# All five engines in written order, and attention reordered into a pipeline of four stages

## The chip, the cores and the metric

The kernel runs on one core of one Trainium2 chip. A core has a matrix engine (TensorE, PE in the profile, with its weight loads as PEld), a vector engine (VectorE, DVE), a scalar engine (ScalarE, ACT), a general engine (GpSimd, POOL) and a queue engine that issues transfers (SyncE, SP). The metric is device time in microseconds (us), lower is better.

## The reference

Windowed attention with a few global keys and a distance bias, followed by a mixture of experts in which each token goes to one expert.

```python
B, H, S, D = 4, 8, 768, 64                 # n_global 8, n_local 96, all fp32
scores = q @ k.T / sqrt(D)
rel = pos[:, None] - pos[None, :]
is_global = pos[None, :] < n_global
is_local = (rel >= 0) & (rel < n_local)
keep = is_global | is_local
dist = where(is_global & ~is_local, n_local, abs(rel))
scores = where(keep, scores - slopes[h] * dist, -1e9)      # slopes[h] = 2 ** -(h + 1)
a = exp(scores - max); a = a / (sum(a) + 1e-9)
x = (a @ v) as (3072 tokens, 512)

logits = x @ w_gate                        # 8 experts
e = argmax(logits); g = softmax(logits)[e]
out[token] = g * (relu(x[token] @ w1[e]) @ w2[e])          # 512 -> 1024 -> 512
```

## The kernel before

**Attention** (`banded`) goes over 24 blocks of 128 queries, six for each of the four batches. Only the keys of the same block and of a mixed tile (96 keys of the block before and 32 global ones) can matter, so a block needs two 128 by 128 score tiles for each of eight heads. For block n, `scores` makes 16 matmuls in two groups of PSUM (`sp`, the array split into halves of 64 rows), VectorE adds the bias (`p<-sp`) and ScalarE takes the exponential. `prep_q` and `prep_k` transpose the next block's q and k on TensorE through a PSUM tile `pt`, and ScalarE copies out `qt`, VectorE `kt`; GpSimd then builds the mixed key tile `ka`. `values` multiplies with v (`po`, 64 columns), ScalarE copies `ot`; sums and gate logits go into `pr` (`one_in` and `gate_w` matmuls, 32 columns), ScalarE copies `rs`; `px` and a transposed `rs` bring the result to tokens as rows; VectorE divides by the sums and writes the rows `xr`. The PSUM tiles `pt` and `px` take turns in two buffers (tag "t").

The loop's order is: `scores(n)`, `prep(n+1)`, `values(n-1)` with its transposes at once. After six blocks `choose` picks an expert for every token, `dispatch` turns that into row numbers with twelve small matmuls, and GpSimd scatters the rows into a table in DRAM by indirect transfers.

**Bias tiles**: VectorE makes distance and mask for three 128 by 128 forms, seven operations each, and then for each form and head one more (L317, 24 in all).

**Experts**: the first 128 tokens of an expert are handled by `up_s` and `down_s`, the rest by one `pass` per expert, whose width (a multiple of 32) is chosen at run time by a switch. `x_in_s` and `x_in` transpose gathered rows. The weights of experts 0 and 1 are fetched during attention, 4 transfers of 1 MB each; `ys` is the one buffer from which the results of `down_s` are scattered.

**Order**: only TensorE runs in the order in which the code is written (`manual_schedule(engines={PE})`). For the other engines a scheduler places every instruction, by its own estimate of when it can run; an engine still executes its instructions strictly one after the other. `judge` reduces a per-block flag `ok`, which VectorE updates twice in every block, to one number that decides on a general fallback (it is never taken here).

Of the kernel before, what the change touches and what calls it, by code (L numbers as in the profile page):

```python
# [15 lines left out]
PE = mybir.EngineType.PE  # L16
SP = mybir.EngineType.SP
# [3 lines left out]
def kernel(  # L21
# [40 lines left out]


# [4 lines left out]
                   allow_small_or_imprecise_dtypes=True)  # L68
    col = const.tile([P, P], F32, name="col")
    nc.gpsimd.iota(col[:], pattern=[[1, P]], base=0, channel_multiplier=0,  # L70
                   allow_small_or_imprecise_dtypes=True)
    before = const.tile([P, P], BF16, name="before")
    nc.vector.tensor_scalar(before[:], col[:], iota_p[:, 0:1], None, ALU.is_gt)
    ones = const.tile([P, P], BF16, name="ones")
    nc.vector.memset(ones[:], 1.0)
# [7 lines left out]
    wg = const.tile([P, NDC, E], F32, name="wg")  # L83
    nc.scalar.dma_start(out=wg[:], in_=moe_w_gate.rearrange("(c p) e -> p c e", p=P))


    words = const.tile([P, 2, 2], I32, name="words")
    nc.scalar.dma_start(out=words[:, 0, :], in_=n_global.bitcast(I32).partition_broadcast(P))
    nc.scalar.dma_start(out=words[:, 1, :], in_=n_local.bitcast(I32).partition_broadcast(P))
# [11 lines left out]

    ok = const.tile([P, H], F32, name="ok")
    okn = const.tile([P, 3], F32, name="okn")
    nc.vector.tensor_scalar(okn[:, 0:1], ng, float(GW), None, ALU.is_le)
    nc.vector.tensor_scalar(okn[:, 1:2], nl, float(LW), None, ALU.is_le)
    nc.vector.scalar_tensor_tensor(okn[:, 2:3], nl, 1.0, okn[:, 1:2], ALU.is_ge, ALU.mult)
    nc.vector.tensor_tensor(okn[:, 0:1], okn[:, 0:1], okn[:, 2:3], ALU.mult)
    nc.vector.tensor_copy(out=ok[:], in_=okn[:, 0:1].to_broadcast([P, H]))  # L110
# [50 lines left out]
    def choose(pool, rt, xr, lg):  # L161
# [13 lines left out]
        se = pool.tile([P, NBLK], F32, tag="se", name="se")  # L175
        nc.vector.tensor_reduce(se[:], sh[:], AX.X, ALU.add)
        nc.vector.tensor_scalar(se[:], se[:], 1e-9, None, ALU.add)
        nc.vector.reciprocal(xr[:, :, DM:DM + 1], se[:].unsqueeze(2))
        nc.vector.tensor_copy(out=xr[:, :, DM + 1:DM + 2].bitcast(I32), in_=rt.tokid[:].unsqueeze(2))
        nc.vector.tensor_scalar(rt.tokid[:], rt.tokid[:], S, None, ALU.add)  # L180
        return oh

    def dispatch(pool, pr, rt, xr, oh):
# [52 lines left out]
    def banded(stack, rt, pool, rows, psum, prefetch, early):  # L236
# [170 lines left out]
        def at(n, fn):  # L407
            later.setdefault(n, []).append(fn)
# [657 lines left out]
```

## Time and profile before

| | us |
|---|---|
| median of 3 runs (lowest to highest) | 625.49 (623.59 to 627.94) |
| the profiled execution, whole | 626.1 |
| its span, first to last instruction | 624.2 |
| PE busy in it | 550.9 (88%) |
| DVE, ACT, POOL busy | 175.6, 125.7, 111.1 |
| mean granted clock of TensorE | 0.958 of full speed |

The span has three stages. Attention lasts until about 212 us, with the first second-block matmuls at 21.85. From 212.92 the small form of experts 0 and 1 runs while the last batch's tokens are scattered and gathered. The passes go from 251.71 to 602.6, and some 21 us of last scatters and closing follow. PE is the busiest engine in all of them. How to read it: the other engines' shares say little, since each works for PE and waits for it; what counts is where PE itself stands still, or runs at a lower clock.

### The profile page before, as it was taken

The numbers are of one execution on the slowest core, as the hardware profiler recorded it, in microseconds if no ns is written. First come the engines' busy times: TensorE is split into PE (matmuls) and PEld (weight loads), VectorE is DVE, ScalarE is ACT, GpSimd is POOL, SyncE is SP. The second block draws the span as 40 slices with busy tenths as digits, with TensorE's granted clock in tenths as the row PEclk, the third lists the DMA queues.
The fourth block names the chain that finished last, engine by engine and source line by source line (L and its number), as shares of the span: only waits on it lengthen the run. The fifth ranks groups of instructions, "written<-read, shape, count | busy, mean of one in ns | idle before, by whom it ended". The sixth has DMA issues, their size and how long they took to land. (4 is left out here: it accounts for less than half of the span.)

```text
span 624.2 us, 11099 instructions
## 1 busy us (share of the span) xinstructions
PE 550.9 (88%) x4544; PEld 440.1 (71%) x4544; DVE 175.6 (28%) x514; ACT 125.7 (20%) x237; POOL 111.1 (18%) x155
## 2 busy tenths in 40 slices
PE   3599869889859896899999999999999999999950
PEld 3588758778748674566777788678788777877750
DVE  5765635655736420102001101102101102101010
ACT  1245324334324210110020110011110111121100
POOL 2010410230240336101200301300400300100210
PEclk9999879899989899799999999999999999999995
DMA  9999987665651365131503604503603500100100
GB/s 161 228 246 241 285 232 165 155 186 132 153 162 36 135 238 152 32 129 47 195 18 136 227 18 148 213 18 135 228 18 136 191 18 1 44 1 4 58 24 5
DMA packets 98779, 77.25 MB, mean 124 GB/s; under 512 B 79690, under 2 KB 79690, under 8 KB 98640
## 3 DMA queue, kind: packets, MB, share of 16 engines
q1 hardware_dynamic: 88640, 52.44, 30.5%
q0 software_dynamic: 7040, 18.99, 9.0%
q10 hardware_dynamic: 2960, 4.23, 2.1%
q8 instruction: 56, 0.92, 0.6%
q14 instruction: 83, 0.68, 0.3%
HBM read 60.92 MB, written 14.73 MB: 121 GB/s over the span
## 5 line engine op out<-in xcount | busy, mean ns | idle before, releaser
L891 PE MATMUL ph<-xT,w 128*128 128x288 f32 (+3 forms) x512 | 121.8, 399 | 6.8 <-DVE xT L870 6.8
L898 PE MATMUL py<-hT,w 128*128 128x288 f32 (+3 forms) x512 | 121.3, 393 | 0.0
L891 PEld LDWEIGHTS ph<-xT,w 128*128 128x128 f32 x512 | 95.2, 193 | 34.0 <-DVE xT L870 7.0
L898 PEld LDWEIGHTS py<-hT,w 128*128 128x128 f32 x512 | 92.3, 190 | 21.4
L786 PE MATMUL ph<-xsT,w 128*128 128x128 f32 x512 | 61.6, 281 | 6.4 <-issue 5.5
L786 PEld LDWEIGHTS ph<-xsT,w 128*128 128x128 f32 x512 | 60.0, 196 | 8.3 <-issue 5.2
L348 ACT ACTIVATE p<-p 128x1024 f32<-128x1024 f32 (+1 forms) x48 | 47.0, 983 | 88.9 <-DVE p L347 88.6
L915 DVE TENSOR_TENSOR y<-t,gate 128x256 f32<-128x256 f32 (+2 forms) x32 | 14.3, 446 | 152.7 <-PE t L912 118.9
L797 PE MATMUL py<-w,hsT 128*128 128x512 f32 x128 | 56.4, 592 | 0.0
L893 ACT ACTIVATE hT<-ph 128x288 f32<-128x288 f32 (+3 forms) x64 | 25.5, 398 | 150.6 <-PE ph L891 148.3
L725 POOL DMA_INDIRECT xg<-xs_dram,grow x24 | 24.5, 1020 | 157.1 <-PE py L898 150.2
L336 PE MATMUL sp<-qt,kt 64*128 64x128 f32 x448 | 40.5, 292 | 10.9 <-DVE p L347 7.2
L347 DVE SCALAR_TENSOR_TENSOR p<-sp,other 128x1024 f32<-128x1024 f32 x40 | 47.2, 1214 | 2.1 <-PE sp L336 2.1
L732 POOL DMA_INDIRECT out_dram<-y,to x24 | 23.9, 996 | 123.8 <-DVE y L915 99.0
L336 PEld LDWEIGHTS sp<-qt,kt 64*128 64x128 f32 x448 | 33.6, 203 | 12.4 <-issue 11.7
L797 PEld LDWEIGHTS py<-w,hsT 128*128 128x128 f32 x128 | 23.6, 190 | 26.3 <-issue 26.3
L870 DVE COPY xT<-t 128x512 f32<-128x512 f32 x24 | 15.6, 683 | 90.6 <-PE t L869 90.6
L358 PE MATMUL po<-p,vt 128*64 128x128 f32 x448 | 39.0, 285 | 0.0
L900 ACT COPY yT<-py 128x288 f32<-128x288 f32 (+3 forms) x32 | 12.3, 386 | 118.7 <-PE py L898 118.7
L358 PEld LDWEIGHTS po<-p,vt 128*64 128x64 f32 x448 | 28.1, 143 | 0.9 <-issue 0.8
L225 PE MATMUL pt<-ident,raw_k 128*128 128x128 f32 x96 | 16.5, 299 | 13.8 <-issue 13.7
L358 PE MATMUL po<-p,va 128*64 128x128 f32 x256 | 27.4, 295 | 0.0
(153 smaller groups left out, 495.8 us busy)
## 6 DMA issues: line engine op xcount, KB each, us to landing
w<-in_moe_w_dram SPq DMA_DIRECT2D x28, 1024.0 KB, 6.8
raw_q<-in_q_dram SPq DMA_DIRECT2D x24, 256.0 KB, 4.2
raw_k<-in_k_dram SPq DMA_DIRECT2D x24, 256.0 KB, 4.8
vt<-in_v_dram SPq DMA_DIRECT2D x24, 256.0 KB, 4.3
w<-in_moe_w_dram ACTq DMA_DIRECT2D x4, 1024.0 KB, 6.1
va<-vt SPq DMA_DIRECT2D x16, 192.0 KB, 4.1
va<-vt SPq DMA_DIRECT2D x16, 64.0 KB, 3.5
xs_dram<-xr,slot_i POOLq DMA_INDIRECT x24, 4.7
```

Of the source, the lines that this page charges most:

```text
L225: nc.tensor.transpose(pt[:, m, :], src[:, 2 * m:2 * m + 2, :].rearrange("p a d -> p (a d)"), ident[:])
L336: nc.tensor.matmul(sp[:, a, j, t, :], lhsT=kt[r, 2 * g + j, :], rhs=qts[n][r, 2 * g + j, :], start=True, stop=True, skip_group_check=True)
L347: nc.vector.scalar_tensor_tensor(z, sc, QS, bi, ALU.mult, ALU.add)
L348: nc.scalar.activation(z, z, AF.Exp)
L358: nc.tensor.matmul(po[D * a:D * a + D, m, :], lhsT=vt[:, 2 * m + a, :], rhs=ps[n][m // 2][:, a, m % 2, t, :], start=(x == 0), stop=(x == l ...
L725: nc.gpsimd.indirect_dma_start(out=dst.bitcast(I32), out_offset=None, in_=xs_dram[:], in_offset=bass.IndirectOffsetOnAxis(ap=idx, axis=0), ...
L732: d = nc.gpsimd.indirect_dma_start(out=out[:], out_offset=bass.IndirectOffsetOnAxis(ap=idx, axis=0), in_=src, in_offset=None, bounds_check ...
L786: nc.tensor.matmul(ph[:, i, :], lhsT=self.w[e % 3][0][:, c, ts(f, P)], rhs=self.xsT[e % 2][:, c, :], start=(c == 0), stop=(c == NDC - 1), ...
L797: nc.tensor.matmul(py, lhsT=self.hsT[:, f, :], rhs=self.w[e % 3][1][:, f, :], start=(f == 0), stop=(f == NFC - 1), skip_group_check=True)
L891: nc.tensor.matmul(ph, lhsT=w1t[:, c, ts(f, P)], rhs=xT[:, c, 0:n], start=(c == 0), stop=(c == NDC - 1), skip_group_check=True)
L893: nc.scalar.activation(hT[:, f, 0:n], ph, AF.Relu)
L898: nc.tensor.matmul(py, lhsT=w2t[:, f, ts(d, P)], rhs=hT[:, f, 0:n], start=(f == 0), stop=(f == NFC - 1), skip_group_check=True)
```

## The change

All five engines now run in written order, and the code is written for that:

- Attention: `values` is cut in two. In iteration n TensorE does `scores(n)`, the transposes of q and k of block n+1, the transposes of the results of block n-2 (`tokens`), then the value, sum and gate matmuls of block n-1. Everything of one array split stands together, and `rs` and `ot` are transposed one iteration after they were made.
- `dispatch` of a batch comes one iteration after `choose`, in a spare part of `pr`; the reciprocals and token numbers (`gates`) are written just ahead of it. `xsT` of expert 0 is made in the last iteration.
- q is scaled when it is copied out of PSUM, so the bias is added by a plain add. Distances come from four operations on all three forms at once, and the per-head tiles `other` and `first` from ScalarE and GpSimd. Block 0 uses the distance directly.
- Loads run three blocks ahead (three buffers). The weights of experts 0 and 1 come in sixteen pieces of 512 KB, one per iteration from the seventh on.
- Two `ys` buffers; in a pass `x_in_s` of the next small form comes earlier and `x_meta` last; half of `down_s(1)` comes after the transposes of pass 0; `ok` is worked out in `judge`, from sums kept in `den_all`.

```diff
+    fast.enter_context(tc.manual_schedule(engines={PE, ACT, DVE, POOL, SP}))
...
-            transposed(ps_t, qts[n][:], rawt[n]["q"], "act")
+            transposed(ps_t, qts[n][:], rawt[n]["q"], "act", QS)
...
+        dist = bias.tile([P, 3, P], F32, name="dist")
+        BIG = NEG / slopes[H - 1]
+        nc.vector.tensor_scalar(dist[:], rel, nl, None, ALU.is_ge)
+        nc.vector.scalar_tensor_tensor(dist[:], key, ng, dist[:], ALU.is_ge, ALU.mult)
+        nc.vector.tensor_scalar(rel, rel, nl, None, ALU.min)
+        nc.vector.scalar_tensor_tensor(dist[:], dist[:], BIG, rel, ALU.mult, ALU.add)
...
+                if on == "act":
+                    nc.scalar.activation(dst, src, AF.Copy, bias=0.0, scale=-slopes[h])
+                else:
+                    nc.gpsimd.tensor_scalar(dst, src, -slopes[h], None, ALU.mult)
...
-                nc.vector.scalar_tensor_tensor(z, sc, QS, bi, ALU.mult, ALU.add)
+                    nc.vector.tensor_tensor(z, sc, bi, ALU.add)
...
+        feed = [load_ for e in range(NS) for load_ in ex.fetches(e, parts=4)]
+        rs = {}
         for n in range(N + 1):
             if n < N:
                 scores(n)
-                if n + 2 < N:
-                    load(n + 2)
-                if n == 2 * NBLK:
-                    prefetch()
             if n + 1 < N:
                 prep_q(n + 1)
+            if n < N:
+                exps(n)
+            if n == 0:
+                biases(1, (0, 1, 2, 3), "act")
+            if n == 2:
+                biases(0, range(H), "act")
+                ex.clear_s()
+            if n + 1 < N:
                 prep_k(n + 1)
                 mix_v(n + 1)
-            for fn in later.pop(n, ()):
-                fn()
+            if n + 3 < N:
+                load(n + 3)
+            if n >= NBLK and feed:
+                feed.pop(0)()
+            b, i = divmod(n - 2, NBLK)
+            if n >= 2:
+                if i == 0 and b:
+                    xr, _, oh, gates = seqs[b - 1]
+                    gates()
+                    dispatch(pool, prs[n - 2][:, 2, :], rt, xr, oh)
+                if i == 1 and b == B - 1:
+                    ex.early()
+                tokens(n - 2, rs.pop(n - 2))
+            if n == N:
+                ex.x_in_s(0, ps_t.tile([P, NPAIR, P], F32, tag="t", name="pt"))
             if n:
-                values(n - 1)
...
-            self.ys = T([P, DM], F32, name="ys")
+            self.ys = [T([P, DM], F32, name=f"ys{i}") for i in range(2)]
...
                     if e + 1 < E:
-                        self.x_meta(e + 1)
                         more.append(lambda: (self.x_in(e + 1, 0), self.x_in(e + 1, 1)))
+                        more.append(lambda: self.x_in_s(e + NS) if e + NS < E else None)
                         more.append(lambda: None)
-                        more.append(lambda: self.x_in(e + 1, 2))
-                    if e + NS < E:
-                        more.append(lambda: self.x_in_s(e + NS))
+                        more.append(lambda: (self.x_in(e + 1, 2), self.x_meta(e + 1)))
...
-        ex.x_in_s(0)
-        for half in range(2):
-            ex.up_s(0, half)
+        ex.up_s(0, 0)
         dispatch(pool, ex.turn("t")[:].rearrange("p t c -> p (t c)"), rt, xr, oh)
+        ex.up_s(0, 1)
         ex.table()
         ex.gathers(0)
+        ex.x_in_s(1)
         ex.gathers(1)
-        ex.x_in_s(1)
...
-        for half in range(2):
-            ex.down_s(1, half)
-        ex.x_meta(0)
+        ex.down_s(1, 0)
         for t in range(TP):
             ex.x_in(0, t)
+        ex.x_meta(0)
+        ex.down_s(1, 1)
...
+            nc.vector.tensor_tensor(okn[:, 0:1], okn[:, 0:1], ex.over[:], ALU.mult)
+            ok = const.tile([P, 2, B * NBLK * H], F32, name="ok")
+            den, rden = (den_all[:, i].rearrange("p n h -> p (n h)") for i in range(2))
+            nc.vector.tensor_scalar(ok[:, 0], den, 1.0e30, None, ALU.is_le)
+            nc.vector.tensor_scalar(ok[:, 1], rden, 20.0, None, ALU.is_le)
```

On TensorE, the end of one attention iteration before the change (the transposes of q and k, then values, sums and gates, then `px` and `rs`, then the next scores); what an instruction waits for stands in brackets:

```order
L225 MATMUL pt<-ident,raw_k 128x128 [waits DMAHW7_49,DVE_49,PE_49]
L358 MATMUL po<-p,vt 64x128 x13
L369 MATMUL pr<-p,one_in 32x128 x15
L374 MATMUL pr<-ot,gate_w 32x128 [waits Activation_49]
L380 MATMUL px<-ident,ot 128x128 [waits PE_49]
L381 MATMUL pr<-ident,rs 128x128 [waits Activation_49]
L336 MATMUL sp<-qt,ka 128x128 [waits DVE_49,Pool_49]
```

and with the change, where the same engine has:

```order
L239 MATMUL pt<-ident,raw_k 128x128 [waits DMAHW6_49,PE_49]
L414 MATMUL pr<-ident,rs 128x128 [waits Activation_49]
L417 MATMUL px<-ident,ot 128x128 [waits Activation_49]
L387 MATMUL po<-p,vt 64x128 x13
L398 MATMUL pr<-p,one_in 32x128 x15
L403 MATMUL pr<-ot,gate_w 32x128 [waits Activation_49]
L358 MATMUL sp<-qt,ka 128x128 [waits Pool_49]
```

The transposes of `rs` and `ot` moved from behind the gates to behind the transposes of k, and `px` now waits for ScalarE.

On VectorE in the second half of the second batch, before the change (`tokid` is the token number that `choose` writes into the rows of a batch):

```order
L347 SCALAR_TENSOR_TENSOR p<-sp,other 128x1024 x2
L230 COPY kt<-pt 128x512
L179 COPY xr<-tokid 128x6 [waits DMASW3_49,DMASW4_49,DMASW2_49,DMASW5_49,DMASW1_49,DMASW0_49]
L180 TENSOR_SCALAR tokid<-tokid 128x6 [waits DVE_49]
L389 TENSOR_SCALAR den<-pr 128x8
```

and with the change, where the same write stands in the dispatching iteration:

```order
L244 COPY kt<-pt 128x512
L189 TENSOR_REDUCE se<-sh 128x6
L190 TENSOR_SCALAR se<-se 128x6
L191 RECIPROCAL xr<-se 128x6
L192 COPY xr<-tokid 128x6
L193 TENSOR_SCALAR tokid<-tokid 128x6
L210 TENSOR_TENSOR rk<-pr,base_e 128x48
```

The copy of the token numbers moved behind the reciprocals of its own batch and waits for no transfer any more.

On VectorE between pass 6 and pass 7, before the change (`bad_i` is the flag of `judge`, made from the TensorE matmul L1023):

```order
L800 TENSOR_SCALAR ys<-py_2931,gates 128x512 [waits DMASW5_49,PE_49,Activation_49]
L1024 TENSOR_SCALAR bad_i<-t_2935 128x1 [waits PE_49]
L1061 SWITCH_STRIDE
```

and with the change:

```order
L856 TENSOR_SCALAR ys_140<-py_2825,gates 128x512 [waits PE_49,Activation_49]
L1071 TENSOR_SCALAR okn<-num 128x1
L1075 TENSOR_TENSOR okn<-okn,over 128x1 [waits DVE_49]
L1078 TENSOR_SCALAR ok<-den_all 128x192
L1081 TENSOR_REDUCE bad<-ok 128x1 [waits DVE_49]
L1085 CAST bad_b<-bad 128x1 [waits DVE_49]
L1088 TENSOR_SCALAR bad_i<-t_2828 128x1 [waits PE_49]
```

Eleven operations moved here from earlier places. TensorE's matmul of `judge` (L1087, which reads `bad_b`) still stands right ahead of pass 7.

## Rows read from the trace of the kernel before

**Rows 1.** Busy time by stretch: length, engines busy, clock, DMA share, GB/s.

```profile
251.71:602.60 350.89, 345.10 (x1700) 270.21 (x1700) 42.31 (x109) 44.97 (x108) 47.99 (x48) 0.99 0.25 90
60.00:80.00 20.00, 18.11 (x293) 15.19 (x289) 11.90 (x35) 8.94 (x16) 7.59 (x10) 0.91 0.99 287
```

**Rows 2.** Timeline of the start: start, length, engine, line, [idle before, releaser].

```profile
7.07 0.16 DVE L99 TENSOR_TENSOR num<-num,part_f 128x2 f32<-128x2 f32 x1
...
11.21 1.71 DVE L317 SCALAR_TENSOR_TENSOR first<-m_dist,m_neg 128x128 f32<-128x128 f32 x8
...
21.85 3.79 PE L336 MATMUL sp<-qt,kt 64*128 64x128 f32 x32 [7.19 <-DVE p L347]
...
29.58 0.49 PE L336 MATMUL sp<-qt,ka 64*128 64x128 f32 x4
```

**Rows 3.** PE's waits up to 255 us: total, times, longest.

```profile
PE pt L225 <- issue: 13.7, 3, 6.7
PE sp L336 <- DVE p L347: 7.2, 1, 7.2
PE ph L891 <- DVE xT L870: 6.8, 1, 6.8
PE pr L187 <- DVE oh L173: 5.7, 3, 1.9
```

**Rows 4.** Timeline of one block and the start of the next.

```profile
102.22 0.49 PE L336 MATMUL sp<-qt,ka 64*128 64x128 f32 x4
...
103.84 2.35 DVE L347 SCALAR_TENSOR_TENSOR p<-sp,other 128x1024 f32<-128x1024 f32 x2
...
104.21 0.66 PE L225 MATMUL pt<-ident,raw_q 128*128 128x128 f32 x4
...
105.23 0.44 PE L358 MATMUL po<-p,va 128*64 128x128 f32 x4
...
107.13 1.08 PE L369 MATMUL pr<-p,one_in 128*32 128x128 f32 x32
...
108.10 0.43 PE L374 MATMUL pr<-ot,gate_w 128*32 128x128 f32 x8
108.45 0.42 PEld L380 LDWEIGHTS px<-ident,ot 128*128 128x128 f32 x4 [0.20 <-issue]
...
109.23 1.16 PE L336 MATMUL sp<-qt,kt 64*128 64x128 f32 x16
...
110.32 0.66 PE L225 MATMUL pt<-ident,raw_q 128*128 128x128 f32 x4
...
111.07 0.60 ACT L228 ACTIVATE qt<-pt 128x512 f32<-128x512 f32 x1 [2.16 <-PE pt L225]
```

**Rows 5.** Timeline around the first long PE stall in attention.

```profile
85.89 0.17 DVE L179 COPY xr<-tokid 128x6 int32<-128x6 int32 x1 [8.54 <-DMA xs_dram<-xr,slot_i]
```

**Rows 6.** Timeline from the first expert matmul to pass 0.

```profile
212.92 9.04 PE L786 MATMUL ph<-xsT,w 128*128 128x128 f32 x64 [0.82 <-DVE xsT L775]
...
221.79 0.19 PE L187 MATMUL t<-oh,before 128*128 128x48 bf16 x1
...
241.01 0.23 DVE L874 TENSOR_TENSOR to<-xg,inv_i 128x3 int32<-128x3 int32 x1 [10.62 <-DMA xg<-xs_dram,grow]
...
249.12 0.75 DVE L800 TENSOR_SCALAR ys<-py,gates 128x512 f32<-128x512 f32 x1 [7.80 <-DMA out_dram<-ys,tos]
...
251.71 22.17 PE L891 MATMUL ph<-xT,w 128*128 128x352 f32 x64 [6.79 <-DVE xT L870]
...
262.09 0.47 ACT L893 ACTIVATE hT<-ph 128x352 f32<-128x352 f32 x1 [1.90 <-PE ph L891]
```

**Rows 7.** Waits from 255 us on: total, times, longest.

```profile
PE ph L786 <- issue: 5.5, 6, 1.0
```

**Rows 8.** Timeline at the start of pass 7.

```profile
583.75 0.75 DVE L800 TENSOR_SCALAR ys<-py,gates 128x512 f32<-128x512 f32 x1 [2.94 <-PE t L1023]
```

More of the change, by code (lines that the diff above doesn't have):

```diff
@@ L81 @@
                    allow_small_or_imprecise_dtypes=True)
[L83 to L89, printed above, removed]
+    ahead = const.tile([P, 3, P], F32, name="ahead")
+    nc.vector.tensor_scalar(ahead[:], rel, 0.0, FAR, ALU.is_lt, ALU.mult)
+    nc.vector.tensor_tensor(rel, rel, ahead[:], ALU.max)
+    before = const.tile([P, P], BF16, name="before")
+    nc.vector.tensor_scalar(before[:], col[:], iota_p[:, 0:1], None, ALU.is_gt)
+    ones = const.tile([P, P], BF16, name="ones")
+    nc.vector.memset(ones[:], 1.0)
     part_i = const.tile([P, 3, 2], I32, name="part_i")
@@ L281, in prep_k @@
                 kas[n + 1] = t[:]
-        load(0)
-        load(1)
+        for n in range(3):
+            load(n)
         gate_w = bias.tile([P, NPAIR, GW], F32, name="gate_w")
@@ L310, in banded, with biases @@
+        nc.vector.tensor_scalar(rel, rel, nl, None, ALU.min)
+        nc.vector.scalar_tensor_tensor(dist[:], dist[:], BIG, rel, ALU.mult, ALU.add)
         first = bias.tile([P, 2, 2, 2, P], F32, name="first")
         other = bias.tile([P, 2, 2, 2, 2, P], F32, name="other")
-        for t in range(3):
-            _, dist, neg = mask(mpool, rel[:, t, :], key[:, t, :], P)
-            for h in range(H):
+        def biases(which, heads, on):
+            for h in heads:
                 g, j, a = h // 4, h // 2 % 2, h % 2
-                out_ = first[:, g, a, j, :] if t == 0 else other[:, g, a, j, t - 1, :]
-                nc.vector.scalar_tensor_tensor(out_, dist[:], -slopes[h], neg[:], ALU.mult, ALU.add)
@@ L330, in scores @@
                 for j in range(2):
-                    for t, kt in enumerate((kas.get(n), own)):
+                    m = 2 * g + j
+                    for t, kt in enumerate((kas.get(n), kts[n][:])):
                         if kt is None:
@@ L377, in values, with tokens @@
             nc.scalar.copy(rs[:], pr[:, 0, :])
+            del ps[n]
+            return rs
+        def tokens(n, rs):
+            b, i = divmod(n, NBLK)
+            pr, ot = prs.pop(n), ots.pop(n)
+            nc.tensor.transpose(pr[:, 1, :], rs[:], ident[:])
             px = ps_t.tile([P, NPAIR, P], F32, tag="t", name="px")
@@ L720, in fetch @@
                 s_ = src[e].rearrange("(c p) f -> p c f", p=P)
[L721 to L722 removed]
+                for a in range(0, n, n // parts):
+                    r = slice(a, a + n // parts)
+                    yield lambda dst=dst, s_=s_, r=r: queue.dma_start(out=dst[:, r, :], in_=s_[:, r, :])
+        def fetch(self, e, queue=nc.sync):
+            for load in self.fetches(e, queue):
+                load()
         def gather(self, dst, idx):
```

224 lines of the change are left out of this document (115 added, 109 removed).

## Prediction, written before the changed kernel ran

> **What bounds the kernel now.** I read the busy times first, by engine and by stretch: PE is the busiest engine everywhere, and in the passes it is busy for 345.10 of 350.89 us [rows 1]. So almost nothing can be won there, and I looked for the time in which PE stands still or runs slowly. The table of PE's waits up to 255 us gives it [rows 3]: 13.7 us in three waits ahead of the transposes of k, 7.2 once for the bias of the first blocks, 6.8 ahead of pass 0, 5.7 in three waits for the choice of experts. The timelines then say why. In the three 13.7 us waits the releaser is only "issue", but VectorE stands still beside them: it sits in a copy of token numbers that waits for the scatter of an earlier batch [rows 5], or in a read of gathered rows; the copies and adds behind it are ready, but VectorE takes its instructions one by one. The 6.8 us ahead of pass 0 are of the same kind: VectorE waits 7.80 us until the one `ys` buffer has been scattered, with the copies of `xT` behind it [rows 6]. So the kernel is bound by PE, plus some 33 us in which other engines hold PE up, plus the slow clock after such a stall.
>
> **The start.** Before, the second block's scores begin at 21.85 and the third's at 29.58 [rows 2]. With the change VectorE has, after n_local is known at 7.23, a small copy (0.2), the copy of `kt` (about 0.7; ScalarE's copy of that size takes 0.60 [rows 4]), four operations of 384 columns, eight of 128 columns for block 0, and the copy of the next `kt` (0.7). A 128-column operation takes 1.71/8 = 0.21 [rows 2], a 1024-column one 2.35/2 = 1.18 [rows 4], so 384 columns are about 0.48 and the four 1.9; the eight read PSUM, and I take 2.3 rather than 1.71. That is 7.2 + 0.2 + 0.7 + 1.9 + 2.3 + 0.7 = 13.0, and PE starts at about 13.2. The per-head tiles lie beside that on ScalarE and GpSimd: no row has their price, but by the 0.60 of a 512-column copy four are at most 2.4 and ScalarE is done at about 15, when the first add wants them; if they took twice as long, the start would be 2 us later. Before, block 1 took 29.58 - 21.85 = 7.7 with PE at half speed at first; now it has no results to transpose, I take 6.8. Third block at 20.0: **9.6 us won** (7 to 11).
>
> **A block in steady state.** Before, a block takes 109.23 - 102.22 = 7.0: scores 1.99, transposes of q and k 1.02, values 1.90, sums 0.97, gates with the switch behind them 0.35, `px` and `rs` 0.78 [rows 4]. Sixteen scores take 1.99 and eight 110.32 - 109.23 = 1.09, so a matmul of 128 columns is 0.112. Now thirteen transposes stand in a row: 1.02 for eight and the switch behind them, 0.56 for five more. 1.99 + 1.58 + 1.90 + 0.97 + 0.35 = 6.8. But `px` takes the buffer from which ScalarE has just to copy `qt`. That copy begins 111.07 - 110.32 = 0.75 after the transposes do and takes 0.60 [rows 4], so `px` can't begin before about 1.40, where the nine transposes ahead of it are over at 1.0: 0.4 us of waiting, in every block. **A block is 7.2, longer than before.** VectorE's part (two adds 2.35, `kt` 0.7, tokens 1.6) and ScalarE's (0.6, two exponentials of 1.05, 0.6, 0.3) fit.
>
> The trace marks 0.20 us of idle weight loading at the switch from gates to `px` [rows 4]. The Trainium skill, in "TensorEngine Tiling (Array Packing)", section "Tiling Modes", says that a change of tiling mode drains the engine. The new order has one such change less in a block, and by that alone a block would come to 6.8; the sum goes by 7.2, and 6.8 is the first rival.
>
> **Blocks that differ.** The first block of a batch has half the scores: 6.35. In the second the choice stands on VectorE behind the tokens: adds done at 3.45 after the block's start, `kt` 4.15, tokens 5.7, the difference that ScalarE exponentiates 6.2. ScalarE's copy of `ot` is queued behind that exponential, and the gate matmuls wait for `ot`: ready at 7.15 instead of 5.55, so this block is 7.5. In the third, ten more operations of VectorE (gates and dispatch, 2 us) stand ahead of the tokens, PE waits some 0.65 for `pr` and has the twelve small matmuls, 0.4: 8.3. A batch is 6.35 + 7.5 + 8.3 + 3 x 7.2 = 43.8. The waits of 13.7 and 5.7 us go altogether: the token copy and the read of gathered rows now stand where their transfers were over long before. From the third block on: 8.4 (eight bias tiles on ScalarE ahead of `ot`), 3 x 7.2, 3 x 43.8, 0.9 for the nine operations of `early`, and 6.0 from the last iteration to the first expert matmul (with two waits of some 0.5 for `rs`): 168.3, against 212.92 - 29.58 = 183.3. **15.0 us won**; the first expert matmul is at 188.3.
>
> **To pass 0.** Before 251.71 - 212.92 = 38.8 [rows 6]. Now PE has `up_s(0)` 7.2 (64 matmuls at 0.112; 9.04 before, at half speed in part), dispatch 0.4, four transposes 0.6 with their switch, `down_s(0)` 7.2 (as many columns), `up_s(1)` 7.2, half of `down_s(1)` 3.6, twelve transposes for pass 0 1.4, the other half 3.6: 31.2. It must not wait for the gathers: from dispatch to landed rows it was 241.01 - 221.79 = 19.2; dispatch is now at 3.6, so they land at 22.8, and PE wants them at 26.2. That is 3.4 us of cover; were it gone, each us beyond would count. With two `ys` buffers nothing waits for a scatter, and the copies of `xT` lie under the second half. **7.6 won.**
>
> **Passes.** Pass 0 began slowly: ScalarE takes one product each 0.47 + 1.90 = 2.37 us, so the third should have been ready at 251.71 + 7.1 + 0.2 = 259.0 and was at 262.09: 3.1 won. `x_in_s` earlier hides the copy of `xsT` for which PE waited 5.5 us in six places [rows 7]: 5.5 won. Against that stands `judge`. PE's matmul of `judge` is ahead of pass 7 and needs VectorE's flag. Before, the flag was there long before, and VectorE's last `ys` came only behind that matmul [rows 8]. Now VectorE does `ys` (0.75) and eleven small operations (0.15 to 0.55, 2.5 together): PE stands 3.3 us, and then I take 1.7 for a slow clock (0 to 3.1, as at pass 0). **3.6 won.** The tail of 21.6 us stays.
>
> **Sum.** 9.6 + 15.0 + 7.6 + 3.6 = 35.8 off the profiled execution's 626.1 gives 590.3; that execution is 0.6 over the median of the runs, so 589.7. I say 590.
>
> **Rivals.**
>
> *No wait for `qt`* (PE finds the buffer free): 6.8 a block, 0.4 less in some twenty blocks, 582. For it: the switch saved is real. Against it: the transposed `px` shares its buffer with q in every iteration, and ScalarE can't be quicker than its own 0.60.
>
> *The clock.* New short stalls (1.6 us in the choosing blocks, 0.65 in the dispatching ones) bring the half clock back. In the 20 us that hold the first dispatch and its 1.9 us wait the granted clock was 0.91 [rows 1], which is 1.8 us; six such and more at the start make 11: 601.
>
> *Transfers*, the one that ends slower than before. From the seventh iteration on each block moves three loads of 256 KB, 256 KB of mixed v, a piece of 512 KB and a sixth of six scatters of 264 KB, 1.8 MB in all. At the 287 GB/s that the full queues moved at 60 to 80 us [rows 1] this is 6.4 us and fits in a block. Three buffers put the loads some 21 us ahead. In sixteen blocks of 7.3 it would take 7.3 + (21 + 36)/16 = 10.9 us per block to lose all that is won, which is 169 GB/s; below that rate the change loses. At 160 GB/s it ends at about 636. Against it: pieces are half as large, so a load waits less behind one, and the stalls before were VectorE's, not the transfers'.
>
> *It gives back what it wins*: what now is late in place of the stalls (gathers for pass 0, mixed keys behind scatters on GpSimd) takes 30 us: 620. The cover of 3.4 us above and a whole iteration for the mixed keys speak against it.
>
> **How the numbers follow.** Forecast 0.58, no wait for `qt` 0.20, clock 0.15, given back 0.04, transfers 0.03. The forecast's own terms leave some 8 us on either side (start 7 to 11, judge 3.3 to 6.4, odd blocks); with the two nearest rivals the range is 576 to 604. A change under 1% can't be told from none here. Faster by over 1%: 0.93, the same 0.04, slower 0.03.
>
> **What would show it.** PE's first long run of scores at about 13 instead of 21.85; no wait of 5 us or more on PE before pass 0; blocks of 7.2 with a wait for ScalarE ahead of `px`; the first expert matmul near 188 and pass 0 near 219; none of the six waits of 1 us ahead of `up_s`; one new wait of some 3 us for VectorE ahead of pass 7. It would be wrong if PE waits for transfers from the seventh block on, if the per-head tiles are late, or if the granted clock in attention is below 0.95.

## The result, and the profile after

The changed kernel takes 607.57 us (median of 4 runs, 605.6 to 609.5) against 626.41 of the kernel before in the same comparison: ratio 0.970, 95% interval 0.966 to 0.975. It is faster, by half of what was forecast (590, range 576 to 604). The profiled execution, 609.5 us as a whole, has a span of 607.60 us. One condition has to be known to read the later numbers: two of the sets of kernels that were measured side by side ran while TensorE issued its matmuls slowly behind every burst of scatters, whatever the kernel; they are marked, and are compared only with each other.

These are the windows of the changed kernel, cut at the four places that the forecast named (start of the third block's scores, first expert matmul, pass 0, TensorE's last work). A row gives the stretch, its length, the busy time of TensorE, its weight loads, VectorE, ScalarE and GpSimd, then TensorE's granted clock, the DMA share and GB/s:

```profile
18.85:196.45 177.60, 157.11 (x2548) 135.18 (x2544) 106.33 (x247) 73.81 (x124) 32.43 (x55) 0.96 0.80 189
196.45:231.18 34.73, 32.06 (x189) 24.00 (x189) 10.84 (x38) 2.39 (x4) 20.90 (x22) 0.95 0.50 172
231.18:586.15 354.97, 345.49 (x1700) 271.98 (x1700) 43.73 (x120) 44.97 (x108) 48.85 (x49) 0.99 0.28 95
```

So the start took 18.85 (forecast 20.0), attention 177.6 (168.3), the way to pass 0 34.7 (31.2). The passes took 355.0, 4.1 more than before [rows 1] where 3.6 less was forecast. The profiled execution was to take 590.3; its shortfall of 19 us is 9.3 + 3.5 + 7.7, less 1.1 won at the start. All of TensorE's waits above 0.5 us in the changed kernel:

```profile
PE ph L947 <- issue: 8.8, 3, 3.5
PE pr L414 <- DVE base_e L217: 8.6, 3, 2.9
PE pr L403 <- ACT ot L391: 5.6, 5, 1.4
PE pt L239 <- DMA raw_q<-in_q_dram: 4.7, 1, 4.7
PE px L417 <- ACT qt L242: 3.6, 18, 0.2
PE t L1087 <- DVE bad_b L1085: 3.1, 1, 3.1
PE ph L842 <- DVE xr L434: 2.4, 1, 2.4
PE pr L414 <- ACT rs L406: 0.9, 2, 0.4
PE sp L358 <- DVE kt L244: 0.9, 1, 0.9
```

Every wait of [rows 3] and the six of [rows 7] are gone. In their place stand four that the forecast had (0.2 for `qt`, 18 times; 3.1 for the flag of `judge`; 1.4 for `ot` in the blocks that choose; two of 0.4 for `rs`), one that it had much smaller (`base_e`, 8.6 in three), and two that it didn't have at all: 8.8 us in three waits ahead of passes, marked "issue", and 2.4 for the rows of x. The waits for `raw_q` and `kt` belong to the start. The timeline around the first of the three dispatches in attention:

```profile
54.06 2.06 PE L358 MATMUL sp<-qt,kt 64*128 64x128 f32 x32
...
61.09 0.43 PE L403 MATMUL pr<-ot,gate_w 128*32 128x128 f32 x8 [1.39 <-ACT ot L391]
61.45 0.49 PE L358 MATMUL sp<-qt,ka 64*128 64x128 f32 x4
...
64.52 0.29 PE L207 MATMUL pr<-oh,ones 128*128 128x8 bf16 x6
64.93 0.68 DVE L244 COPY kt<-pt 128x512 f32<-128x512 f32 x1
65.53 0.19 DVE L189 TENSOR_REDUCE se<-sh 128x6 f32<-128x48 f32 x1
...
67.46 0.16 DVE L217 TENSOR_TENSOR base_e<-base_e,pr 128x8 f32<-128x8 f32 x1
67.67 0.33 PE L414 MATMUL pr<-ident,rs 128*128 128x128 f32 x1 [2.86 <-DVE base_e L217]
...
68.70 3.25 PE L387 MATMUL po<-p,vt 128*64 128x128 f32 x32
...
73.11 0.49 PE L358 MATMUL sp<-qt,ka 64*128 64x128 f32 x4
...
80.22 0.49 PE L358 MATMUL sp<-qt,ka 64*128 64x128 f32 x4
```

The block that chooses lasts 61.45 - 54.06 = 7.39, the one that dispatches 73.11 - 61.45 = 11.66, the next 7.11. (The other two that dispatch last 11.66 and 12.92.) TensorE is ready for the transposition of `rs` (L414) at 64.8. It writes the second plane of `pr`, whose third plane VectorE reads until 67.62, at the end of ten operations that follow the copy of `kt`. When it goes on, 32 products take 3.25 us (2.96 and 3.68 behind the other two dispatches) where they take 1.97 in an experiment below that has no such stall. Their granted clock, last but two in the row, is 0.59, between the levels of 1.2 GHz (0.5) and 2.4 GHz (1.0):

```profile
68.70:71.95 3.25, 3.25 (x37) 3.08 (x40) 0.87 (x3) 0.00 (x0) 2.33 (x4) 0.59 0.88 320
```

TensorE ahead of pass 0, and ahead of pass 7, with VectorE's part of `judge`:

```profile
224.91 3.60 PE L853 MATMUL py<-w,hsT 128*128 128x512 f32 x8
231.18 9.05 PE L947 MATMUL ph<-xT,w 128*128 128x352 f32 x24 [2.67 <-issue]
...
557.84 0.75 DVE L856 TENSOR_SCALAR ys<-py,gates 128x512 f32<-128x512 f32 x1 [2.95 <-PE py L853]
...
560.64 0.16 DVE L1085 CAST bad_b<-bad 128x1 bf16<-128x1 f32 x1
560.85 0.16 PE L1087 MATMUL t<-bad_b,ones 128*128 128x1 bf16 x1 [3.11 <-DVE bad_b L1085]
564.55 11.47 PE L947 MATMUL ph<-xT,w 128*128 128x160 f32 x64 [3.54 <-issue]
```

Pass 0 begins 2.67 us after TensorE's last matmul (224.91 + 3.60), though VectorE's copies of `xT` ended at 226.1. Pass 7 waits first 3.11 for the flag, as forecast, and then 3.54 more.

### The profile page after: what moved, and what is told of

It is laid out like the page before. It is cut to its first block, busy times and chain, and to the rows that moved or that the text cites. A ratio compares the mean times of both kernels' runs of the same rounds, so it can differ in the third digit from the quotient of the medians.

```text
span 607.6 us, 11043 instructions
## 1 busy us (share of the span) xinstructions
PE 546.7 (90%) x4544; PEld 440.7 (73%) x4544; DVE 171.8 (28%) x434; ACT 128.9 (21%) x249; POOL 114.1 (19%) x160
## 5 line engine op out<-in xcount | busy, mean ns | idle before, releaser
L947 PE MATMUL ph<-xT,w 128*128 128x288 f32 (+3 forms) x512 | 123.1, 403 | 8.8 <-issue 8.8
L947 PEld LDWEIGHTS ph<-xT,w 128*128 128x128 f32 x512 | 97.1, 197 | 39.6 <-issue 17.4
L372 DVE TENSOR_TENSOR p<-sp,other 128x1024 f32<-128x1024 f32 x40 | 47.1, 1219 | 57.7 <-PE sp L358 57.7
L379 ACT ACTIVATE p<-p 128x1024 f32<-128x1024 f32 (+1 forms) x48 | 44.6, 978 | 2.1 <-DVE p L372 2.0
L387 PE MATMUL po<-p,vt 128*64 128x128 f32 x448 | 41.1, 299 | 0.0
L387 PEld LDWEIGHTS po<-p,vt 128*64 128x64 f32 x448 | 30.2, 152 | 1.7 <-issue 1.7
L776 POOL DMA_INDIRECT xs<-xs_dram,grow_s x8 | 8.1, 1011 | 123.7 <-issue 98.6
L300 POOL COPY ka<-kt 128x384 f32<-128x384 f32 x16 | 8.1, 508 | 119.6 <-DVE den_all L423 93.2
L219 POOL DMA_INDIRECT xs_dram<-xr,slot_i x24 | 23.7, 989 | 16.0 <-issue 6.1
```

The source lines that it names most:

```text
L219: d = nc.gpsimd.indirect_dma_start(out=xs_dram[:], out_offset=bass.IndirectOffsetOnAxis(ap=slot_i[:, u:u + 1], axis=0), in_=xr[:, u, :].bi ...
L372: nc.vector.tensor_tensor(z, sc, bi, ALU.add)
L379: nc.scalar.activation(z, z, AF.Exp)
L387: nc.tensor.matmul(po[D * a:D * a + D, m, :], lhsT=vt[:, 2 * m + a, :], rhs=ps[n][m // 2][:, a, m % 2, t, :], start=(x == 0), stop=(x == l ...
L947: nc.tensor.matmul(ph, lhsT=w1t[:, c, ts(f, P)], rhs=xT[:, c, 0:n], start=(c == 0), stop=(c == NDC - 1), skip_group_check=True)
```

## The experiments

The changed kernel was measured twice, and serves as the control: 0.970 (above) and 0.965 in a later comparison. All ratios are to the kernel before, measured beside it. A difference between two ratios of different comparisons is worth less than one within a comparison: the two controls are 3 us apart.

**The control.** 

> The changed kernel itself, as a control on the chip of this call. Theory (the slow issue of matmuls after the scatters belonged to the chip of the last call): without such waits 0.968 to 0.973 of the kernel before, with them 0.99 to 1.00. Rival (it belonged to the edits): 0.968 to 0.973 here, and the edited kernels of this call again show the slow issue.

Measured: 603.57 us, ratio 0.965 (0.960 to 0.970). No slow issue, and the same waits as above to 0.3 us, but 8.1 instead of 8.8 for the three ahead of passes, and 0.8 for k at the start.

**Dispatch behind the values.**

```diff
-                if i == 0 and b:
-                    xr, _, oh, gates = seqs[b - 1]
-                    gates()
-                    dispatch(pool, prs[n - 2][:, 2, :], rt, xr, oh)
...
                 rs[n - 1] = values(n - 1)
+            if n >= 2 and i == 0 and b:
+                xr, _, oh, gates = seqs[b - 1]
+                gates()
+                dispatch(pool, prs[n - 1][:, 2, :], rt, xr, oh)
```

> The gates and the dispatch of the earlier batch are emitted behind the values of the iteration, into the sums' tile of the next block, instead of ahead of the tokens. Theory (the dispatching block is the term that was too small): the transposition of the sums no longer stands behind VectorE's ten operations, so the three waits of 2.87 us for base_e go, and with them the slow matmuls that follow (32 products with v took 3.25 and 3.68 us where they take 1.9 to 2.0 elsewhere). That is 3 x 2.9 = 8.6 us and 3 x 1.4 to 2.5 us of clock, 12 to 15 us in all: 593 to 596 us. Rival (VectorE's work is the bound there, wherever it stands): the adds to the next scores come 2 us later, PE waits for the exponentials instead, and the time stays within 3 us of 607.6.

Measured: 599.71 us, 0.959 (0.955 to 0.963). The three waits for `base_e` are gone, but the gain, 4 to 7 us by the controls, is only about half of what the theory gave. One new wait came up in the last batch:

```profile
166.63 0.16 POOL L804 IOTA pl<- 128x3 f32 x1
166.83 0.18 DVE L806 TENSOR_TENSOR loc<-pl,lim 128x24 f32<-128x24 f32 x1 [4.44 <-POOL pl L804]
...
167.57 0.22 DVE L428 TENSOR_TENSOR lh<-pr,den_all 128x64 f32<-128x64 f32 x1
167.94 1.93 PE L398 MATMUL pr<-p,one_in 128*32 128x128 f32 x32 [4.77 <-DVE lh L428]
```

`early` reads a row of indices that GpSimd makes behind the six scatters of the dispatch, which now stand just ahead of it; VectorE waits for GpSimd, and TensorE for VectorE.

**The same, with the index row made at the start.** The iota moves from `early` to `clear_s`.

```diff
             nc.gpsimd.memset(self.lim[:], float(P))
+            self.pl = self.pool.tile([P, TP], F32, name="pl")
+            nc.gpsimd.iota(self.pl[:], pattern=[[P, TP]], base=0, channel_multiplier=1,
+                           allow_small_or_imprecise_dtypes=True)
```

> As the dispatch behind the values, and in addition the index row that the early gathers read is made by GpSimd at the start instead of behind six scatters. Theory (with the dispatch moved, the last batch's early gathers made VectorE wait 4.44 us for GpSimd's row and PE 4.77 us for VectorE, and that took back a third of the gain): both waits go, no wait of PE above 1.5 us is left between 20 and 185 us, and the time falls by another 5 to 8 us, to 0.945 to 0.952 of the kernel before. Rival (VectorE or GpSimd is short of time there whatever stands ahead): a wait of 3 us or more for VectorE stays in the last batch, and the ratio stays at 0.957 to 0.960.

Measured: 595.51 us, 0.951 (0.947 to 0.955): 14 to 20 thousandths below the controls, 9 to 12 us. Both waits are gone. Attention, from the third block's scores at 19.79 to the first expert matmul at 184.93, takes 165.1 us instead of 177.6, less than the forecast's 168.3, and each of the three blocks that dispatch takes 7.98. In the block that dispatches the first batch, the timeline and the window of the products have

```profile
65.30 0.27 PE L414 MATMUL pr<-ident,rs 128*128 128x128 f32 x1
66.36 1.97 PE L387 MATMUL po<-p,vt 128*64 128x128 f32 x32
```

```profile
66.36:68.33 1.97, 1.97 (x37) 1.80 (x40) 1.83 (x8) 1.25 (x2) 0.80 (x3) 1.00 1.17 246
```

so here, with no stall ahead of them, the products run at a granted clock of 1.00. What was not tried is to leave the dispatch where it stood and give it a tile of its own.

**The exponential of the choice behind the copies.**

```diff
-        nc.scalar.activation(sh[:], sh[:], AF.Exp)
+        def raised():
+            nc.scalar.activation(sh[:], sh[:], AF.Exp)
...
                 rs[n - 1] = values(n - 1)
+            if n >= 2 and i == NBLK - 1 and b < B - 1:
+                seqs[b][3].raised()
```

> In three of the four batches ScalarE's exponential of the choice is issued behind the copies of the values instead of ahead of them. Theory: the wait of the gate matmuls for the copy of ot, 1.39 us three times, goes, 4 us, and no more than 1 us of clock: 603 to 604 us. Rival (the dispatch, one iteration later, waits for VectorE anyway and takes up what is won): the wait of the sums' transposition for base_e grows from 2.9 towards 4 us and the time stays within 1.5 us of 607.6.

Measured: 604.64 us, 0.968 (0.965 to 0.971). The waits for `ot` fall from 5.6 to 2.0 us in the list and the three for `base_e` stay at 2.9, so the rival's mechanism didn't occur. But the time lies between the two controls: a gain of 3.6 us can't be told from none here.

**Judge ahead of pass 0.** VectorE's operations of `judge` stand behind `table`, its matmul behind `up_s(1)`; `passes` gets an empty function.

```diff
-        ex.passes(judge)
+        ex.passes(lambda: None)
```

> The operations of judge stand behind table and its matmul behind the second small product, ahead of pass 0, where VectorE has nothing to do for 10 us; nothing of judge is left ahead of pass 7. Theory: the 3.1 us for the flag go, and of the 2.4 us that pass 7 runs longer than before (21.5 against 19.1 us) at least half; the wait of 3.5 us marked issue behind it stays if it is a wait for code: 602 to 604 us. Rival (the wait marked issue is a consequence of PE's standing still): it goes too, 598 to 600 us. If VectorE's sixteen operations in their new place hold up the copies for pass 0, PE waits there and the time is 607.

Measured: 598.65 us, 0.960 (0.957 to 0.963), 3 to 7 us below the controls. The wait for the flag and the one behind it are both gone, the rival's case: pass 7 follows the small product without a gap.

```profile
551.66 3.60 PE L853 MATMUL py<-w,hsT 128*128 128x512 f32 x8
555.10 8.86 PE L947 MATMUL ph<-xT,w 128*128 128x160 f32 x64
```

Its 64 products take 8.86 us, at a granted clock of 1.00, instead of 11.47 at 0.77. The two waits ahead of passes 0 and 6 stay (2.67 and 1.98). What the 3.54 us may have been is seen in the DMA view, which lists what each transfer queue moved (packets, MB, share). In the changed kernel from 560.8 to 567.7, behind the wait for the flag, and in this one from 548 to 555.1, while the small product still runs, the instruction queue that moves 16 KB pieces has

```profile
q8 instruction: 2, 0.03, 2.1%
```

and

```profile
q8 instruction: 2, 0.03, 2.2%
```

In the changed kernel it has nothing from 549 to 560.8, one piece between 562 and 563, and the other behind 564.6, when pass 7 has begun. So code came only after TensorE was past the wait for the flag. That the queue is TensorE's and the piece pass 7's is read from these times; no view names them. The Trainium skill says of this, in "Runtime: NRT & Kernel Launch", section "Instruction fetch mechanics", that a taken branch whose target isn't in the fetched window forces a fetch before execution can go on. The times of the two pieces are in keeping with it, but no view shows which code lies in the window, and passes 1 to 5, entered by the same switch, have no such wait. Nor does the flag always bring the 3.54 us: the two runs with 1 MB pieces, below, are one program with and without them.

**Where the code lies.** 64 matmuls of one row and one column ahead of the first transposes.

```diff
+        pad = ps_o.tile([P, NPAIR, P], F32, tag="o", name="pad")
+        for _ in range(64):
+            nc.tensor.matmul(pad[0:1, 0, 0:1], lhsT=ones[:, 0:1], rhs=ones[:, 0:1], start=True, stop=True)
```

> 64 matmuls of one row and one column stand ahead of the first transposes, where PE waits for q; they move all of PE's later code by 128 instructions and compute nothing. Theory (the waits marked issue ahead of passes 0, 6 and 7 are waits for PE's own code after a branch, and which of them show depends on where a pass lies in the code that is fetched 16 KB at a time): the three waits of 2.7, 2.6 and 3.5 us change: some go, others may come ahead of other passes; the time moves by 2 to 9 us either way. Rival (they belong to the place: the engine's queue runs empty there, or it waits for another engine that the trace doesn't name): the same three waits of the same lengths, and 607 to 608 us.

Measured: 603.8 us, 0.966 (0.962 to 0.970), which is that of the controls. The wait ahead of pass 6 is gone; those ahead of 0 and 7 are 2.49 and 3.95. So in this run one of the three changed with the place of the code, as the theory had it, and two stayed; the time didn't move clear of the controls.

**The hint ahead of pass 0**, left out, and moved 7 us up (`load_forms` and `hint(0)` ahead of `up_s(1)`).

> The hint for the branch into pass 0 is left out; nothing else. Theory (the code of pass 0 comes only when PE reaches the branch, and the hint did nothing for it: one 16 KB piece of instructions was moved between 226 and 231 us): the wait marked issue ahead of pass 0 stays between 2.3 and 3.0 us. Rival (the hint brings part of the code): it grows to 4 us or more.

Measured: one run of 608.9 us; the wait ahead of pass 0 is 2.70. In this run the hint's absence changed nothing.

> The load of the forms and the hint for pass 0 stand ahead of the second small product's first half instead of behind both halves, 7 us earlier. Theory (the hint doesn't matter): the wait ahead of pass 0 stays between 2.3 and 3.0 us, and no more than 1 us is lost to the earlier load. Rival (the hint came too late): the wait goes or falls below 1 us, and a 16 KB piece of instructions is moved between 210 and 222 us.

Measured: one run of 604.84 us, and no wait ahead of pass 0: the theory fell, the rival's held in this run. What follows takes part of that back.

**Five edits together**: dispatch behind the values, index row, exponential, judge, and in the last block `x_rows` ahead of `choose`.

> Together: dispatch behind the values, the index row early, the exponential of the choice behind the copies, judge ahead of pass 0, and in the last block the rows of x ahead of the choice. Theory (the gap between forecast and result is the sum of these waits and their slow clock): 3 x 2.87 and 3 x 1.39 and 3.1 and 3.5 and 1 us of waits, some 6 to 8 us of clock, together 26 to 28 us off 607.6: 580 to 582 us, which is 0.928 of the kernel before. Rival (each removal uncovers the next wait, as the early gathers did): 0.94 to 0.95, some 590 us.

Measured: 579.91 us, 0.929 (0.924 to 0.934).

> The five edits, once more beside the control. Theory: 0.927 to 0.932 where the control has 0.968 to 0.973, 40 us of difference in thousandths of the kernel before either way. Rival (a chip with the slow issue takes more from this kernel than from the control): less than 25 thousandths of difference.

Measured beside the second control: 577.36 us, 0.926 (0.922 to 0.930), 26 us below the control's 603.57. Its 0.926 is 39 thousandths below the control's 0.965 (the expectation's 40 are thousandths, not us). Its waits of 2 us and more, and its windows from the third block's scores (19.21) to the first expert matmul (179.47) and on to pass 0 (209.85):

```profile
PE pt L245 <- DMA raw_q<-in_q_dram: 4.7, 1, 4.7
PE px L423 <- ACT qt L248: 4.2, 21, 0.2
PE ph L952 <- issue: 2.4, 1, 2.4
PE pr L409 <- ACT ot L397: 2.0, 5, 1.1
```

```profile
19.21:179.47 160.26, 151.50 (x2548) 130.01 (x2544) 104.09 (x242) 73.36 (x123) 30.80 (x54) 1.00 0.89 209
179.47:209.85 30.38, 30.38 (x190) 22.65 (x190) 13.23 (x54) 2.63 (x5) 20.66 (x21) 1.00 0.49 166
```

In both stretches the granted clock is 1.00, the level of 2.4 GHz, and both are now shorter than forecast (168.3 and 31.2). These two executions of one program also differ: the first has a wait of 2.35 us ahead of pass 0, the second none. TensorE's last matmul ahead of the pass ends at 210.8 and 210.0. In the first the 16 KB instruction queue moved nothing from 204 to 210 us, in the second one piece. So whether the code comes in time is not settled by the program alone, and the one run of the earlier hint proves little.

> The five edits and the hint for pass 0 ahead of the second small product. Theory (the hint works, and nothing else changed): 2 to 3 us less than the five edits alone. Rival (the load of the forms, which now stands behind judge's matmul and ahead of the product, costs as much): within 1 us of them.

Measured: 578.18 us, 0.926 (0.923 to 0.930), the same as without it, and no wait ahead of pass 0 in either. The earlier hint can't be told from no change.

**The small product's transposes last**, as before.

```diff
-                        more.append(lambda: self.x_in_s(e + NS) if e + NS < E else None)
                         more.append(lambda: None)
                         more.append(lambda: (self.x_in(e + 1, 2), self.x_meta(e + 1)))
+                        more.append(lambda: self.x_in_s(e + NS) if e + NS < E else None)
```

> The changed kernel with the transposes of xs last in each pass. Theory: 5.6 us in six waits come back in front of the small product, 0.978 to 0.980 where the control has 0.970. Rival (the late place costs three times that by a way not seen): 0.99 or more beside a control of 0.970.

Measured beside the control: 608.5 us, 0.975 (0.971 to 0.980) against 0.965, and the six waits are back:

```profile
PE ph L842 <- issue: 5.6, 6, 1.0
```

**The two sets with the slow issue.** In the first of them:

> All five edits and the earlier hint for pass 0. Theory (the hint must stand far enough ahead of its branch): the wait marked issue ahead of pass 0, 2.35 us, goes, the one ahead of pass 6 stays, and the time falls by 2 to 3 us, to 0.923 to 0.926 of the kernel before. Rival (with judge's matmul ahead of it, the load of the forms now holds PE up, or the hint's effect hung on where the code lay): no change from 0.9286, and a wait of 2 us ahead of pass 0 or of the load stays.

Measured: 596.43 us, 0.958 (0.955 to 0.962), where the same program without the slow issue has 0.926.

> The changed kernel with the transposes of xs behind the last ones of xg in each pass, as before, so that the copy of xsT is the last thing ahead of the small product. Theory (the forecast's term of 5.5 us): six waits of 0.9 to 1.0 us ahead of the small product come back, 5.5 us, and the ratio rises to 0.978 to 0.980. Rival (the copies stand in another order on VectorE than before, and the wait was theirs): under 2 us in all.

Measured: 622.59 us, 0.998 (0.995 to 1.001), where the same program has 0.975.

> The kernel of all edits with the earlier hint, and 64 empty matmuls at the start that move PE's later code by 128 instructions. Theory (where a pass lies in the code decides whether its wait shows): the wait of 2.4 us ahead of pass 6 goes, as it did with the empty matmuls alone; whether another comes ahead of some other pass is open; if none does, 2 us less than without them. Rival (the empty matmuls' effect was a coincidence of something else): the wait ahead of pass 6 stays.

Measured: 591.07 us, 0.952 (0.948 to 0.956), 5 us less than without the empty matmuls in this set (the intervals overlap a little), where the theory had 2; no wait ahead of any pass in the list.

> The changed kernel with the weights of the small products in pieces of 1 MB instead of 512 KB, eight blocks long instead of sixteen. Theory (the pieces' size is worth nothing, since no wait for a transfer is seen from the fourth block on): the ratio stays at 0.970, within 0.004, and no wait of PE for q, k or v comes up. Rival (the smaller pieces keep the loads of q and k from standing behind them): waits for raw_q or raw_k of 1 us or more from the seventh iteration on, and 3 us or more in all.

Measured: 620.23 us, 0.997 (0.994 to 1.000). Beside 0.998 of `xs_late` in the same set this can't be read as the price of the pieces. It was run once more, and fell into the other such set:

> The changed kernel with the weights of the small products in pieces of 1 MB. Theory (the size of the pieces is worth nothing): 0.965 to 0.972 of the kernel before, and no wait of PE for q, k or v after 20 us. Rival (the loads of q and k stand behind the larger pieces): waits for them from the seventh iteration on, 0.975 or more.

Measured: 618.85 us, 0.996 (0.992 to 1.000), the slow issue again. Neither run has a wait of TensorE for q, k or v beyond the start. What the piece size is worth stays open.

The two runs of this one program show something else. The wait for the flag ahead of pass 7 is 3.12 us in both. Behind it the first run waits 4.00 us more:

```profile
576.79 1.43 PE L947 MATMUL ph<-xT,w 128*128 128x160 f32 x4 [4.00 <-issue]
```

and the second 0.64:

```profile
568.26 1.96 PE L947 MATMUL ph<-xT,w 128*128 128x160 f32 x6 [0.64 <-issue]
```

In the first the 16 KB instruction queue moved nothing from 560 to 572.6, where the wait for the flag ends, and one piece from there to 576.8. In the second it moved one piece from 557 to 567.4, ahead of the end of that wait (567.47). `xs_late` and `xs_late_again` have 0.65 and 0.63 there. So pass 7's long wait goes with a piece of code that comes late, and the flag alone doesn't make it late.

In that second set one part of the change alone was run, in the kernel before:

```diff
-            self.ys = T([P, DM], F32, name="ys")
+            self.ys = [T([P, DM], F32, name=f"ys{i}") for i in range(2)]
```

> One part of the change alone: the kernel before, with two ys buffers. Theory (beneath the 6.8 us lay the copies of xT and the load of the pass's code): VectorE's copies follow the transposes at once, and PE still waits 2 to 3 us ahead of pass 0, so 4 to 5 us of wait and up to 3 us of clock go: 0.988 to 0.993. Rival (the whole wait goes, as the forecast had it): no wait above 1 us ahead of pass 0, 10 us less: 0.984 or lower.

Measured: 618.56 us, 0.991 (0.987 to 0.995). The wait of [rows 6] ahead of pass 0 falls from 6.79 to 2.82, as the theory had it, and the way from the first expert matmul (211.00) to pass 0 takes 34.7 us instead of 38.8:

```profile
244.96 0.69 DVE L870 COPY xT<-t 128x512 f32<-128x512 f32 x1 [1.40 <-remote]
...
245.71 6.49 PE L891 MATMUL ph<-xT,w 128*128 128x352 f32 x11 [2.82 <-issue]
```

The pass begins 0.06 us after the last copy of `xT` ends, so the copies explain all that is left, and this run can't say whether the code came in time beneath them.

## Why the prediction was wrong

**The start: right**, 10.7 us won for a forecast of 9.6. VectorE's four wide operations take 0.41 to 0.62 each, the eight of block 0 1.67 where 2.3 was taken, and the second block's scores begin at 11.79, 1.4 earlier than forecast.

**The blocks: right but one.** A steady block takes 7.1 (forecast 7.2), with the wait for `qt` in place, 0.2 instead of 0.4; so the first rival (6.8, no wait) fell. Without that wait it would be 6.9, against 7.0 before, where one change of mode more stood in a block. The Trainium skill, in "TensorEngine Tiling (Array Packing)", section "Tiling Modes", says that a change of tiling mode drains the engine. The trace agrees in so far as the weight loads still stand idle for 0.17 to 0.20 us at such changes; that one change less makes a block 0.2 shorter it doesn't show. The first block of a batch takes 6.2 (6.35), the choosing one 7.39 (7.5).

**The step that failed first** is the dispatching block: "ten more operations of VectorE (gates and dispatch, 2 us) stand ahead of the tokens, PE waits some 0.65 for `pr`". The operations and their 2 us are right; the place and so the length of the wait were not. TensorE doesn't come to `pr` only with the sums, behind the values' products; the transposition of `rs`, which the change put ahead of those products, writes the same tile while VectorE still reads it. The prediction's own numbers give that wait: `kt` done at 4.15 and 2 us of operations make 6.15, and TensorE is there at 1.99 + 1.02 + 0.4 = 3.41 (measured from the block's start: 6.17 and 3.36), which is 2.7 us. So the wait is 2.87 and not 0.65, and the products behind it run slowly: 11.66, 11.66 and 12.92 instead of 8.3. That is 11.3 us in three, more than all of attention's 9.3; most other blocks took 0.1 less than forecast. The dispatch experiments show it: without the wait the products take 1.97 and the block 7.98, and with the early index row attention is 12.5 us shorter and the whole time 9 to 12.

The slow clock behind this wait is likely but not certain. In `hint0_early` TensorE stands just as long, and its products run at 1.00:

```profile
69.97 0.33 PE L414 MATMUL pr<-ident,rs 128*128 128x128 f32 x1 [2.87 <-DVE base_e L217]
```

```profile
70.67:72.64 1.97, 1.97 (x37) 1.80 (x40) 1.16 (x4) 0.00 (x0) 1.66 (x2) 1.00 1.07 341
```

In the eight traces that have the wait and no slow issue it comes 24 times; behind 5 of them the 32 products took 1.97, behind 19 of them 2.96 to 3.68. What decides it stays open. Where they take 1.97, in `xs_late_again`, the block is 10.05 long, so the wait alone costs some 2 us and the clock up to 2.9.

**To pass 0** two small terms were missing. The first expert matmul waited 2.42 for the rows of x, which the last block writes behind the choice (a wait of 1.2 is left with the other order). That wait still counts in attention's stretch; behind it the first 32 products took 5.47 us, at a granted clock of 0.69, where they take 3.84 in the five-edit kernel with the early hint. And "the copies of `xT` lie under the second half" was right, but beneath the old wait of 6.8 us lay something else. The changed kernel waits 2.67 us for nothing that the profile names, with one 16 KB piece of instructions moved between 227 and 231.2. That this is pass 0's code is argued, not shown apart: in the five-edit kernel, too, the piece came late in the execution with the wait and earlier in the one without. The forecast had put this term at nothing. The 1.6 us of slow products and these 2.7 are more than the 3.5 that the stretch took too long.

**The passes** won 7.0 us up to the start of pass 5 (472.91 - 231.18 against 500.49 - 251.71 before), the forecast having 8.6 for all: the six waits of [rows 7] went, and came back for 5.6 us in `xs_late_again`, so that term is confirmed. Pass 0 gained 1.3 of the 3.1 forecast (64 products in 20.89 us, 22.17 before), since it again starts behind a stall; in `hint0_early`, without one, they take 19.10, which is the whole 3.1. The term of `judge`, "PE stands 3.3 us, and then I take 1.7 for a slow clock", was right in its first half (3.1) and too small in the second: 3.54 us behind the wait, in which code was loaded, and 2.6 us of slow clock (64 products in 11.47 at a granted clock of 0.77, and in 8.86 at 1.00 without the stall). `judge_early` took all of it away. Another wait of this kind stands ahead of pass 6 (2.60).

**The sum.** The clock rival had the right sign, but gave 601, since it knew only short stalls: attention's granted clock is 0.96 in the changed kernel and 1.00 in the five-edit one. Transfers and the rival that gives all back weren't met. With the five edits 577 to 580 us are reached, below the forecast: what it got wrong were waits that could be taken away.

## What to carry to other kernels

In an engine's written order, look for every tile that an instruction writes and ask who still reads another part of it; a transposition moved to the front takes its wait along. When a wait is removed, list what else lay beneath it (copies, the code behind a branch, a row that a third engine makes behind its queue), since the next latest of them is what remains. Put work whose inputs have long been there, like a final flag, where its engine is idle, never between the last matmul and a branch.

## What the runs showed of the hardware

A wait for an engine just ahead of a branch costs more than itself: 3.1 us for a flag were followed by 3.5 us, in which a 16 KB piece of code was moved, and by 2.6 us of slow clock. It doesn't always: where the piece had come earlier, 0.63 to 0.65 us followed the same wait (three traces). Why a program with the same hint has the wait ahead of pass 0 or 7 in one execution and not in the next stays open.

The slow issue was not expected at all. Behind the scatters of each dispatch TensorE issues one to four matmuls about every 0.7 us for some 4 to 5 us. The five-edit kernel with the early hint has in the set with it (first window, and the timeline) and in the one without (second window)

```profile
70.00:82.00 12.00, 9.00 (x131) 6.68 (x130) 5.25 (x13) 3.29 (x5) 6.82 (x8) 1.00 0.60 197
```

```profile
70.00:82.00 12.00, 11.60 (x184) 10.18 (x182) 8.96 (x20) 5.83 (x8) 6.80 (x8) 1.00 0.73 233
```

```profile
77.79 0.42 PE L404 MATMUL pr<-p,one_in 128*32 128x128 f32 x4 [0.43 <-issue]
...
79.25 0.43 PE L404 MATMUL pr<-p,one_in 128*32 128x128 f32 x4 [0.44 <-issue]
80.70 0.56 PE L404 MATMUL pr<-p,one_in 128*32 128x128 f32 x11 [1.02 <-issue]
```

It costs the five-edit kernel 20 us (0.958 against 0.926 of 623 us) and the changed one with late transposes 14 (0.998 against 0.975). It is not the program, since the same ones ran without it, and not one chip alone, since one of the two chips also ran kernels without it. In the trace of `before_two_ys` it is there too (4.6 us of such waits in the values' products), but the kernel before took 622.86 and 622.17 us in the two sets, no longer than in the others (623.30 to 626.41). So the ratios of these sets make the change look smaller than the others do. Its cause is open.
